# Attention feeding two mixtures of experts: tail scores in two equal parts, the feature map's minimum on GpSimd, and a fused last pair

## The chip, the cores and the metric

The kernel runs on one core of one Trainium2 chip. The metric is the device time of one execution in microseconds (us); the median of three runs of the kernel before is 1090.05 us (1089.28 to 1090.55). PE is the matrix engine, ACT the scalar engine, DVE the vector engine, POOL is GpSimd, and SP issues the transfers.

## The reference

Four batches of eight heads, 576 positions of 64 numbers. Each head mixes local causal attention with a read from a memory matrix; the result, 2304 tokens of 512, goes through two mixtures of experts.

```python
scores = scale * np.matmul(q, k.transpose(0, 1, 3, 2))      # causal mask, softmax -> a
local = np.matmul(a, v)
def phi(x):
    return np.where(x > 0, x, np.exp(x) - 1.0) + 1.0
q_p = phi(q)
mem_out = (q_p @ M_prev) / ((q_p @ z_prev)[..., None] + 1e-06)
x = g * mem_out + (1 - g) * local
# soft mixture: logits = x @ phi; softmax over the tokens -> slots; 8 experts; softmax over the slots -> back
# second mixture: 8 Sinkhorn rounds on the gate, then all 8 experts on all 2304 tokens
```

The feature map phi is x + 1 for positive x and exp(x) otherwise.

## The kernel before

**Stages.** Attention fills the span's first 255 us. It is followed by the first mixture, where weights stream in (255 to 294 us), and by the second, where PE is busy nearly all the time to the end.

**Pairs and steps.** Two heads make a pair; there are 16 pairs, `order[p]` for p = 0 to 15, four to a batch. The 576 queries of a pair are cut in five query tiles: four of 128 and a tail of 64, in which both heads are stacked to fill 128 rows. A step is a pair and a tile. For each step `scores` puts query times key into a bank of the accumulator memory (two products, high and low part of the operands, `kh` and `klz`), takes the smallest of the negated scores with DVE into `mn` and leaves the masked scores in `sm` (L387; the tail's in `smt`, L377), and has ACT exponentiate them in place (L394). `transposes` turns the exponentials on PE (`pt`, L437; the tail's L419 and L425) and ACT or DVE copy them into `pA` (tiles 0 and 1) and `pB` (tiles 2, 3 and the tail). `attend` multiplies them with the values (`po`, L476) and ACT copies the result to `ot`. "sm(2,1)" below is tile 2 of head 1.

**The tail's scores** are made of 576 keys in two parts, 512 and 64 keys wide (L361 to L377).

**The memory read** is prepared one pair ahead. `pre_exp` makes `qe`, the exponential of the raw query `qp` (L330, ACT), and cuts `qp` below at zero (L331, ACT); `pre_phi` adds min(`qe`, 1) to it on DVE (L336). `post_mem` multiplies with the memory (`pma`, `pmb`, L489), `post_mr` and `post_mx` divide. Two pairs ahead, `pre_qh`, `pre_ql`, `pre_kh` and `pre_kl` split queries and keys into high and low parts: the high ones on ACT (`qh`, `kh`), the remainders on POOL (`qh`, `qz`, `klz`, all L268).

**After a pair.** `post_r` makes the divisors of the softmax (`pz`, `sums`, `r`, L522 to L532), `post_x` turns `ot` back and multiplies (L541, L544), `post_add` adds the memory's part on POOL (L556), `post_t` turns x (`pxT`, copies `xT`, L566), and `post_logits` multiplies it with the slots' matrix (`pl`, L579, L585) and adds to `lt` (L592). After the fourth pair of a batch the routing follows: `route_logits` (a maximum, L598), `route_turn`, `route_max`, `route_factor`, and `route_slots` (`pu`, L687; `uacc`, L696). In the last batch `weight_sums` (`rs`, `stkr`, L671 to L674) and `slot_inputs` (`psl`, `sT`, L707) end the stage, and `ph` (L890) begins the first mixture.

**What sets the order.** A hand-written list sets the order on ACT and SP: for each step scores, transposes, attend, with further work put in at a number n of a pair (15 numbers to a pair, `at(p, n, f)`, numbers from `POS`). The table `LATE` holds exponentials back behind a later copy. On PE, DVE and POOL a scheduler sets the order from the same program. `qe` and `xT` share one buffer (tag `sc`).

Of the kernel before, what the change touches and what calls it, by code (L numbers as in the profile page):

```python
# [21 lines left out]
def infini_attention_soft_moe_sinkhorn_moe(  # L22
# [22 lines left out]
    P = 128  # L45
# [66 lines left out]
    with ExitStack() as actx:  # L112
# [18 lines left out]
        nc.vector.memset(zero, 0.0)  # L131
        maskt = e2.tile([P, TAIL], BF16, name="maskt")
        nc.gpsimd.memset(maskt, 0.0)
        for j in range(2):
            sl = maskt[64 * j : 64 * j + 64]
# [131 lines left out]
        def remainder(e, out, x, hi):  # L267
            (nc.gpsimd if e == "P" else nc.vector).tensor_tensor(  # L268
                out=out, in0=x, in1=hi.bitcast(F32), op=ALU.subtract
            )  # L270
# [40 lines left out]
        def pre_kl(X, h, c0=0, c1=S, e=None):  # L311
            X.kl = klz[X.p % 2]
            sl = slice(D * h, D * h + D)
            remainder(
                e or ("DP" if X.p == 1 else CFG["e_kl"])[h], X.kl[sl, h, c0:c1], X.kd[sl, h, c0:c1], X.kh[sl, h, c0:c1]
            )


        def pre_exp(X):
            X.qe = e5.tile([P, S], F32, tag="sc", name="qe")  # L320
# [11 lines left out]
            nc.gpsimd.memset(X.qp[:, S:], 0.0)  # L332

        def pre_phi(X):
            x = X.qp[:, 0:S]
            nc.vector.scalar_tensor_tensor(  # L336
                out=x, in0=X.qe, scalar=1.0, in1=x, op0=ALU.min, op1=ALU.add
            )

# [5 lines left out]

        LATE = {(0, 0): 4, (0, 1): 4, (1, 1): 0, (2, 1): 1, (3, 0): 2, (3, 1): 2}

# [6 lines left out]
        def scores(X, i):  # L354
            last = i == NT - 1
            n = P * (i + 1) if not last else S
            for h in range(1 if last else 2):
                sm = smt if last else e2.tile([P, 4 * P], F32, tag="sm", name="sm", bufs=SMB)
                mnc = X.mn[:, i, h : h + 1]
                if last:  # L360
                    parts = ((0, 4 * P), (4 * P, S))  # L361
                    pss = [pst("ps") for _ in range(2)]
# [11 lines left out]
                    mn2 = X.mn[:, NT, 0:1]  # L374
                    for c, msk in ((0, zero.to_broadcast([P, 4 * P])), (1, maskt)):
# [87 lines left out]
        def attend(X, i):  # L463
# [4 lines left out]
            for n, w, o0 in ((2, 2 * P, 0), (NT, W2, 2 * P)):  # L468
                po = pst("po")
                for j in range(n):  # L470

                    c0 = P * j if n == 2 else P * max(0, j - 2)
                    for h in range(2):
                        t, o_ = (X.pA, 2 * P * j) if n == 2 else (X.pB, OB[j])
                        rhs = t[:, h, o_ : o_ + w - c0]
                        nc.tensor.matmul(  # L476
                            po[64 * h : 64 * h + 64, c0:w], X.vt[:, j, h, :], rhs,
                            start=(j == 0), stop=(j == n - 1),
                        )
                copy(CFG["e_oA" if n == 2 else "e_oB"], X.ot[:, o0 : o0 + w], po[:, 0:w])  # L480


        def post_mem(X):
# [50 lines left out]
        def post_x(X, parts):  # L534
            x1 = X.ot.rearrange("p (t c) -> p t c", t=NT)
            end = X.p == NP - 1
            for t0, t1 in parts:
# [12 lines left out]
                )  # L550
                if end:
                    nc.vector.tensor_add(X.x[:, t0:t1], X.x[:, t0:t1], x1[:, t0:t1])

# [21 lines left out]
        def post_logits(X):  # L575

            pl = pst("pl")
            for t in range(4):
                nc.tensor.matmul(  # L579
                    pl[32 * t : 32 * t + 32, 0:P], phi_sb[:, X.hp],  # L580
                    X.xT[:, P * t : P * t + P], start=True, stop=True,
                )

            for t in range(4):
                nc.tensor.matmul(  # L585
                    pl[32 * t : 32 * t + 32, P : P + TAIL], phi_sb[:, X.hp],
                    X.xT[:, 4 * P : S], start=True, stop=True,
                )
            if X.hp == 0:
                nc.vector.tensor_copy(lt, pl[:, 0 : P + TAIL])  # L590
            else:
# [4 lines left out]
        def route_logits(b):  # L596
            m5 = e4.tile([P, 1], F32, tag="m5", name="m5")
            nc.vector.tensor_reduce(out=m5, in_=lt, op=ALU.max, axis=AX.X)  # L598
            R.m5 = m5

# [75 lines left out]
        def route_slots(b):  # L676
# [7 lines left out]
            for r in range(NHP + 1):  # L684
                for g in range(4):
# [4 lines left out]
                    )  # L690
                if r == 3:
                    weight_sums(b)
# [28 lines left out]
        def at(p, n, f, *args):  # L721
# [4 lines left out]
            ("kh", pre_tiles), ("qh", pre_qh), ("ql0", pre_ql, 0), ("ql1", pre_ql, 1), ("qz", pre_qz), ("kh", pre_kh),  # L726
            ("kl0", pre_kl, 0), ("kl1", pre_kl, 1), ("exp", pre_exp), ("phi", pre_phi),
        )
# [5 lines left out]
        ROUTE = (  # L734
            ("ra", route_logits), ("rb", route_turn), ("rc", route_max), ("rd", route_factor),
            ("re", route_slots),
        )
        for p in range(NP):
# [3 lines left out]
            if p + 1 < NP:  # L742
                if p > 1:
                    at(p, POS["l1"], load_q1, p + 1)
                for nm, f, *a in PRE:
                    if not p or f in (pre_tiles, pre_exp, pre_phi):
                        at(p, POS[nm], f, pairs[p + 1], *a)
            if 0 < p < NP - 2:
                for n, f, *a in ((1, load_heads, "qd"), (2, load_heads, "kd")):
                    at(p, n, f, p + 2, *a)  # L750
            if p < NP - 2:
                for n, f, *a in (
                    (8, pre_qh), (8, pre_ql, 0), (8, pre_ql, 1), (9, pre_qz), (9, pre_kh),
                    (9, pre_kl, 0), (9, pre_kl, 1),
                ):
                    at(p, n, f, pairs[p + 2], *a)
            for n, (nm, f, *a) in enumerate(MEM):
                at(p, POS[nm] if p + 1 < NP else POS["mz"] + 2 * n, f, pairs[p], *a)
            if hp == NHP - 1 and p + 1 < NP:
# [970 lines left out]
```

## Time and profile before

| | |
|---|---|
| median of three runs | 1090.05 us |
| the profiled execution's own time | 1093.55 us |
| its span in the trace | 1091.8 us |
| mean granted clock of PE | 0.987 |
| attention, to the first `ph` | 0 to 254.75 us |
| busy share of the span: PE, POOL, DVE, ACT | 97%, 67%, 72%, 57% |

The shares are a mean over stages of different kinds: outside the attention stage PE alone, or the transfers, set the time, and the change touches only the attention stage and its end. The tail's scores begin once in each pair, so that the distance from one such start to the next is the time of a pair: 13.22 to 13.57 us in the eight pairs that have no routing near them, 15.55 to 16.68 in the three that carry a routing, 13.89 to 14.32 in the three behind those, and 13.39 in the last.

### The profile page before, as it was taken

The page shows a single profiled execution, that of the slowest core. Times are in us where ns is not written, and L with a number is a line of the kernel's source. Part 1 is how long each engine was busy: PE and PEld are TensorE (multiplying, and loading weights), DVE is VectorE, ACT ScalarE, POOL GpSimd, SP SyncE. Part 2 cuts the span into 40 slices and gives each one's busy share as a digit, 9 for nine tenths or more (in the row PEclk, how much of TensorE's full clock was granted, in tenths as well). Part 3 has the DMA queues.
Part 4 walks back from the last instruction along what each step waited for, and adds up shares of the span by engine and source line. Part 5 has one row for each costly group of instructions (what it writes and reads, how often), then busy time and mean ns, then how long its engine had stood idle before and what let it go on. Part 6 is the DMA issues. An engine that isn't in the chain of part 4 may idle for free.

```text
span 1091.8 us, 24586 instructions
## 1 busy us (share of the span) xinstructions
PE 1058.1 (97%) x9157; PEld 968.1 (89%) x9157; DVE 790.7 (72%) x1764; ACT 623.0 (57%) x1322; POOL 730.1 (67%) x683
## 2 busy tenths in 40 slices
PE   6999999988999999999999999999999999999998
PEld 4878878764477899999999999999999999999998
DVE  7888878764157466777777777777777777877776
ACT  7998989841243666456445645554564464456442
POOL 6655646400153499679678867968886796889765
PEclk9999999997989999999999999999999999999999
DMA  9476767568812014113210421321042132110211
GB/s 212 135 216 188 215 202 217 155 235 356 351 55 87 1 20 159 36 20 118 65 24 11 156 39 21 114 67 24 12 155 40 21 113 65 24 16 15 69 54 59
DMA packets 103574, 113.08 MB, mean 104 GB/s; under 512 B 69152, under 2 KB 79520, under 8 KB 99360
## 3 DMA queue, kind: packets, MB, share of 16 engines
q1 hardware_dynamic: 103024, 111.42, 33.8%
q8 instruction: 73, 1.20, 0.5%
q14 instruction: 45, 0.37, 0.1%
q10 hardware_dynamic: 432, 0.09, 0.0%
HBM read 95.74 MB, written 4.72 MB: 92 GB/s over the span
## 4 chain that ended last, share of the span: by engine, by line
PE 80%; DVE 5%; DMA 5%; ACT 4%; issue 3%; POOL 3%; SPq 0%; DVEq 0%; ACTq 0%; POOLq 0%
PE y L1530 56%; PE l L1146 5%; PE po L476 3%; PE pt L437 2%; PE y L1493 2%; DMA kd<-in_k_dram 2%; ACT sm L394 2%; PE pa L1093 2%; DMA wm<-in_moe_w_dram 2%; DMA w<-in_moe_w_dram 1%; PE ph L890 1%; PE ps L371 1%; PE ps L366 1%; DVE sm L387 1%; PE pt L419 1%
## 5 line engine op out<-in xcount | busy, mean ns | idle before, releaser
L1170 DVE SCALAR_TENSOR_TENSOR f<-l,f 128x512 f32<-128x512 f32 x268 | 183.8, 686 | 83.9 <-ACT a11h L1176 70.1
L1187 POOL TENSOR_TENSOR s1l<-f,s1h 128x512 fp32r<-128x512 f32 x67 | 87.3, 1303 | 116.6 <-ACT s1h L1176 116.6
L1544 DVE TENSOR_TENSOR accA<-accA,y 128x512 f32<-128x512 f32 x125 | 85.6, 685 | 54.0 <-PE y L1530 54.0
L1166 ACT ACTIVATE f<-l 128x512 f32<-128x512 f32 x67 | 40.1, 598 | 120.1 <-PE l L1146 119.5
L1176 ACT ACTIVATE a12h<-l 128x512 fp32r<-128x512 f32 x72 | 43.3, 601 | 103.0 <-PE y L1530 83.0
L1187 POOL TENSOR_TENSOR s4l<-f,s4h 128x512 fp32r<-128x512 f32 x67 | 87.7, 1308 | 17.3 <-PE y L1530 17.3
L1544 DVE TENSOR_TENSOR accB<-accB,y 128x512 f32<-128x512 f32 x125 | 85.7, 685 | 4.2
L1187 POOL TENSOR_TENSOR s2l<-f,s2h 128x512 fp32r<-128x512 f32 x67 | 87.6, 1307 | 1.3 <-ACT s2h L1176 0.5
L1187 POOL TENSOR_TENSOR s3l<-f,s3h 128x512 fp32r<-128x512 f32 x67 | 87.8, 1311 | 0.0
L1146 PE MATMUL l<-c4T,a 128*128 128x256 f32 x576 | 78.1, 278 | 0.0
L394 ACT ACTIVATE sm<-sm,mn 128x128 f32<-128x128 f32 (+3 forms) x128 | 70.9, 557 | 8.3 <-DVE mn L387 7.9
L1530 PE MATMUL y<-T2h,s2h 128*128 128x256 f32 x268 | 74.7, 279 | 0.0
L1530 PE MATMUL y<-T2l,s2h 128*128 128x256 f32 x268 | 74.1, 276 | 0.0
L1530 PE MATMUL y<-T2h,s2l 128*128 128x256 f32 x268 | 74.1, 276 | 0.0
L1530 PE MATMUL y<-T1h,s1h 128*128 128x256 f32 x268 | 74.0, 276 | 0.0
L1530 PE MATMUL y<-T1l,s1h 128*128 128x256 f32 x268 | 74.0, 276 | 0.0
L1530 PE MATMUL y<-T1h,s1l 128*128 128x256 f32 x268 | 74.0, 276 | 0.0
L1530 PE MATMUL y<-T4h,a22h 128*128 128x256 f32 x268 | 74.0, 276 | 0.0
L1530 PE MATMUL y<-T4l,a22h 128*128 128x256 f32 x268 | 74.0, 276 | 0.0
L1530 PE MATMUL y<-T4h,a22l 128*128 128x256 f32 x268 | 74.0, 276 | 0.0
L1530 PE MATMUL y<-BB1h,s3l 128*128 128x256 f32 x268 | 73.1, 276 | 0.9 <-POOL s3l L1187 0.9
L1530 PE MATMUL y<-BB2h,a12h 128*128 128x256 f32 x268 | 73.6, 279 | 0.0
(324 smaller groups left out, 4063.1 us busy)
## 6 DMA issues: line engine op xcount, KB each, us to landing
wm<-in_moe_w_dram SPq DMA_DIRECT2D x32, 1024.0 KB, 7.2
raw<-in_moe_w_dram SPq DMA_DIRECT2D x32, 512.0 KB, 3.6
w<-in_moe_w_dram SPq DMA_DIRECT2D x32, 512.0 KB, 5.4
qd<-in_q_dram SPq DMA_DIRECT2D x30, 288.0 KB, 4.2
kd<-in_k_dram SPq DMA_DIRECT2D x30, 288.0 KB, 4.3
c4T<-ct SPq DMA_DIRECT2D x224, 32.0 KB, 2.0
qp<-in_q_dram SPq DMA_DIRECT2D x15, 288.0 KB, 3.0
vt<-in_v_dram SPq DMA_DIRECT2D x16, 256.0 KB, 4.5
```

The source lines that it names most:

```text
L394: nc.scalar.activation(out=sm[:, 0:n], in_=sm[:, 0:n], func=AF.Exp, scale=-1.0, bias=mnc, accum_out=X.sums[:, i, h : h + 1],)
L437: nc.tensor.transpose(pt[:, o_ : o_ + P], pr[:, P * j : P * j + P], ident)
L476: nc.tensor.matmul(po[64 * h : 64 * h + 64, c0:w], X.vt[:, j, h, :], rhs, start=(j == 0), stop=(j == n - 1),)
L1093: nc.tensor.matmul(pa[32 * j : 32 * j + 32, 0:256], soT[:, c, :], w1[j][:, c, :], start=(c == 0), stop=(c == KD - 1),)
L1146: nc.tensor.matmul(ph[:, f, :], a4s[e][:, P * (KH * j + f) : P * (KH * j + f) + P], c4T[:, UT * u : UT * u + UT], start=True, stop=True,)
L1166: nc.scalar.activation(out=f_tile(g, nm), in_=ph(g, nm), func=AF.Relu)
L1170: nc.vector.scalar_tensor_tensor(out=f_tile(g, nm), in0=ph(g, src), scalar=0.0, in1=b, op0=ALU.max, op1=op)
L1176: nc.scalar.activation(out=h_tile(g, nm, "h"), in_=ph(g, nm) if a else FU[g, nm], func=AF.Relu if a else AF.Copy)
L1187: nc.gpsimd.tensor_tensor(out=lo, in0=FU[g, nm], in1=hi, op=ALU.subtract)
L1493: nc.tensor.matmul(Y[g, i], X[g, f"a{i}{j}", "hhl"[n]][:, f, :], BB[j, "hlh"[n]][:, f].rearrange("p a c -> p (a c)"), start=j == 1 and f = ...
L1530: nc.tensor.matmul(o_, a[:, f, :], b[:, f, :], start=n == 0, stop=n == 3 * KH - 1)
L1544: nc.vector.tensor_tensor(out=acc, in0=acc, in1=y, op=ALU.add)
```

## The change

- **Tail scores.** The two parts are 288 keys wide each.
- **Features.** For every pair but the first POOL puts min(`qp`, 0) into `qe` (`pre_min`), ACT exponentiates it in place, and DVE takes the larger of `qp` + 1 and `qe`. ACT's cut at zero (L331) is gone. The remainder `klz` of two pairs ahead moves from number 9 to 14 of a pair.
- **Third step.** sm(2,1) is no longer held back: both heads' exponentials of tile 2 stand together on ACT.
- **The end.** In the last pair the divisors come at number 0; turning `ot` of tiles 0 and 1 back stands inside `attend`; one DVE instruction of 64 columns for each tile and head makes product and sum (`end_x`); the copies of x go to ACT (`end_t`); the products with the slots' matrix are cut in pieces (`end_l`). The maximum of the logits is taken in the instruction that adds them (all batches); the last `weight_sums` moves ahead.

```diff
-                    parts = ((0, 4 * P), (4 * P, S))
+                    parts = ((0, SH), (SH, S))          # SH = S // 2
...
-                nc.scalar.activation(out=X.qe, in_=X.qp[:, 0:S], func=AF.Exp)
-                nc.scalar.activation(out=X.qp[:, 0:S], in_=X.qp[:, 0:S], func=AF.Relu)
+                nc.scalar.activation(out=X.qe, in_=X.qe, func=AF.Exp)
...
+        def pre_min(X):
+            X.qe = e5.tile([P, S], F32, tag="sc", name="qe")
+            nc.gpsimd.tensor_scalar(
+                out=X.qe, in0=X.qp[:, 0:S], scalar1=0.0, scalar2=None, op0=ALU.min
+            )
...
+                nc.vector.scalar_tensor_tensor(
+                    out=x, in0=x, scalar=1.0, in1=X.qe, op0=ALU.add, op1=ALU.max
+                )
...
-        LATE = {(0, 0): 4, (0, 1): 4, (1, 1): 0, (2, 1): 1, (3, 0): 2, (3, 1): 2}
+        LATE = {(0, 0): 4, (0, 1): 4, (1, 1): 0, (3, 0): 2, (3, 1): 2}
...
+                    if n == NT and j == 2 and X.p == NP - 1:
+                        end_x(X, 0, 2)
...
+        def end_x(X, t0, t1):
+            px = pst("px")
+            for t in range(t0, t1):
+                nc.tensor.transpose(
+                    px[:, P * (t - t0) : P * (t - t0) + P], X.ot[:, P * t : P * t + P], ident
+                )
+            for t in range(t0, t1):
+                for h in range(2):
+                    c0 = P * (t - t0) + D * h
+                    xs = X.x[:, t, D * h : D * h + D]
+                    nc.vector.scalar_tensor_tensor(
+                        out=xs, in0=px[:, c0 : c0 + D], scalar=X.r2[:, t, h : h + 1], in1=xs,
+                        op0=ALU.mult, op1=ALU.add,
+                    )
...
+            elif X.hp == NHP - 1:
+                R.m5 = e4.tile([P, 1], F32, tag="m5", name="m5")
+                nc.vector.tensor_tensor_reduce(
+                    out=lt, in0=lt, in1=pl[:, 0 : P + TAIL], scale=1.0, scalar=-3.0e38,
+                    op0=ALU.add, op1=ALU.max, accum_out=R.m5,
+                )
...
-                if r == 3:
+                if r == (0 if b == B - 1 else 3):
                     weight_sums(b)
...
+                for n, f in ((14, pre_min), (15, pre_exp), (15, pre_phi)):
+                    at(p, n, f, pairs[p + 1])
...
-                    (9, pre_kl, 0), (9, pre_kl, 1),
+                    (14, pre_kl, 0), (14, pre_kl, 1),
...
-                    (1, post_r), (2, post_x, ((0, 2),)), (3, post_t, ((0, 2),)),
-                    (3, post_x, ((2, 5),)), (3, post_t, ((2, 5),)), (9, post_logits),
+                    (0, post_r), (1, end_t, 0, 2), (1, end_x, 2, 5), (2, end_l, 0, 2),
+                    (2, end_t, 2, 4), (2, end_t, 4, 5), (3, end_l, 2, 4), (3, end_l, 4, 5),
+                    (9, post_logits),
```

ACT in one pair, before; from the exponentials of tile 0 and 1 to those of tile 3 (`pA` and `pB` are the copies of turned exponentials, `ot` those of the attended values):

```order
L394 ACTIVATE sm,sums<-sm,mn 128x128 x2
L330 ACTIVATE qe<-qp 128x576
L331 ACTIVATE qp<-qp 128x576
L394 ACTIVATE sm,sums<-sm,mn 128x256
L62 ACTIVATE ot<-po 128x256
L62 ACTIVATE ot<-po 128x320
L62 ACTIVATE pA<-pt 128x2x128
L394 ACTIVATE sm,sums<-sm,mn 128x256
L394 ACTIVATE sm,sums<-sm,mn 128x384
L62 ACTIVATE pA<-pt 128x2x256
L394 ACTIVATE sm,sums<-sm,mn 128x384
L62 ACTIVATE pB<-pt 128x3x128
```

The same stretch of ACT now:

```order
L406 ACTIVATE sm,sums<-sm,mn 128x128 x2
L406 ACTIVATE sm,sums<-sm,mn 128x256
L332 ACTIVATE qe<-qe 128x576
L62 ACTIVATE ot<-po 128x256
L62 ACTIVATE ot<-po 128x320
L62 ACTIVATE pA<-pt 128x2x128
L406 ACTIVATE sm,sums<-sm,mn 128x256
L406 ACTIVATE sm,sums<-sm,mn 128x384 x2
L62 ACTIVATE pA<-pt 128x2x256
L62 ACTIVATE pB<-pt 128x3x128
```

The cut at zero is gone, the exponential of the features stands behind one more exponential of scores, and the 512 wide copy to `pA` stands behind the second 384 wide exponential where it stood ahead of it.

POOL in one pair, before:

```order
L268 TENSOR_TENSOR qz_150<-qd,qz_150 64x64 x2
L268 TENSOR_TENSOR qh<-qd,qh 64x512 x2
L268 TENSOR_TENSOR klz_157<-kd,kh 64x576 x2
L343 MEMSET sums 128x2
L556 TENSOR_TENSOR x<-x,ot 128x640
L467 MEMSET ot 128x64
```

And now:

```order
L269 TENSOR_TENSOR qz_150<-qd,qz_150 64x64 x2
L269 TENSOR_TENSOR qh<-qd,qh 64x512 x2
L337 TENSOR_SCALAR qe<-qp 128x576
L269 TENSOR_TENSOR klz_157<-kd,kh 64x576 x2
L355 MEMSET sums 128x2
L606 TENSOR_TENSOR x<-x,ot 128x640
```

The minimum stands between the remainders of the queries and those of the keys, which both come later by its time.

PE at the end of the stage, before, from the last attended values to the logits:

```order
L476 MATMUL po<-pB,vt 64x320 x6
L476 MATMUL po<-pB,vt 64x192 x2
L476 MATMUL po<-pB,vt 64x64 x2
L522 MATMUL pz<-sums,ident 64x1
L541 MATMUL px<-ident,ot 128x128 x2
L566 MATMUL pxT<-ident,x 128x128 x2
L541 MATMUL px<-ident,ot 128x128 x3
L566 MATMUL pxT<-ident,x 128x128 x3
L579 MATMUL pl<-xT,phi_sb 32x128 x4
```

And now (`pz` stands ahead of the first attended values):

```order
L488 MATMUL po<-pB,vt 64x320 x6
L500 MATMUL px<-ident,ot 128x128 x2
L488 MATMUL po<-pB,vt 64x192 x2
L488 MATMUL po<-pB,vt 64x64 x2
L518 MATMUL pxT<-ident,x 128x128
L500 MATMUL px<-ident,ot 128x128 x2
L518 MATMUL pxT<-ident,x 128x128
L500 MATMUL px<-ident,ot 128x128
L525 MATMUL pl<-xT,phi_sb 32x128 x2
L518 MATMUL pxT<-ident,x 128x128 x3
L525 MATMUL pl<-xT,phi_sb 32x128 x2
```

The first two tiles' `px` stands among the last attended values, and the transposes of x are spread among the others.

## Rows read from the trace of the kernel before

**Rows 1.** Busy time by stretch: span, PE, PEld, DVE, ACT, POOL (instructions), clock, DMA share, GB/s.

```profile
100.00:125.00 25.00, 24.07 (x220) 20.24 (x219) 20.34 (x74) 23.25 (x63) 15.66 (x19) 1.00 0.69 205
```

**Rows 2.** Timeline, PE: start us, us, engine, line, operation [idle before <- releaser].

```profile
115.01 0.55 PE L437 MATMUL pt<-ident,sm 128*128 128x128 f32 x3 [0.51 <-ACT sm L394]
115.32 0.71 PE L366 MATMUL ps<-kh,qz 128*128 128x512 f32 x2
...
116.33 0.30 PE L366 MATMUL ps<-kh,qz 128*128 128x64 f32 x2
...
116.69 0.92 PE L489 MATMUL pma<-mbd,qp 128*128 128x130 f32 x6
```

**Rows 3.** Timeline, ACT, the same pair.

```profile
107.05 0.27 ACT L62 ACTIVATE pB<-pt 128x128 f32<-128x128 f32 x1
107.68 0.66 ACT L62 ACTIVATE pB<-pt 128x384 f32<-128x384 f32 x2 [0.36 <-PE pt L419]
...
109.76 0.68 ACT L331 ACTIVATE qp<-qp 128x576 f32<-128x576 f32 x1
...
113.38 0.58 ACT L62 ACTIVATE pA<-pt 128x512 f32<-128x512 f32 x1
114.25 0.61 ACT L394 ACTIVATE sm<-sm,mn 128x384 f32<-128x384 f32 x1 [0.29 <-DVE mn L387]
...
117.02 1.04 ACT L62 ACTIVATE qh<-qd 128x1024 fp32r<-128x1024 f32 x1
```

**Rows 4.** Timeline, POOL, the same pair.

```profile
105.63 2.62 POOL L268 TENSOR_TENSOR qh<-qd,qh 64x512 fp32r<-64x512 f32 x2
108.21 2.90 POOL L268 TENSOR_TENSOR klz<-kd,kh 64x576 fp32r<-64x576 f32 x2
```

**Rows 5.** Timeline, DVE, the same pair.

```profile
108.47 0.41 DVE L387 CUSTOM_DVE_ANT_0 sm<-ps,maskw 128x256 f32<-128x256 f32 x1
...
109.14 0.51 DVE L528 TENSOR_SCALAR r<-sums,gB 128x5 f32<-128x5 f32 x1
110.47 1.25 DVE L336 SCALAR_TENSOR_TENSOR qp<-qe,qp 128x576 f32<-128x576 f32 x1 [0.82 <-ACT qp L331]
```

**Rows 6.** Timeline, DVE and POOL, in a pair that carries a routing.

```profile
97.22 0.76 DVE L336 SCALAR_TENSOR_TENSOR qp<-qe,qp 128x576 f32<-128x576 f32 x1 [1.20 <-ACT qp L331]
...
99.02 0.10 POOL L343 MEMSET sums<- 128x2 f32 x1 [3.17 <-DVE r L528]
```

**Rows 7.** Groups by line and form, POOL, 0 to 320 us: count | busy us, mean ns | idle before.

```profile
L268 POOL TENSOR_TENSOR klz<-kd,kh 64x576 fp32r<-64x576 f32 x29 | 40.9, 1411 | 1.3
...
L332 POOL MEMSET qp<- 128x64 f32 x16 | 2.4, 148 | 1.9 <-PE pmb L489 1.8
...
L880 POOL MEMSET hT<- 128x224 f32 x2 | 0.5, 285 | 20.3 <-PE pu L687 20.3
```

**Rows 8.** The tile qp, its transfers, 0 to 250 us.

```profile
DMA to landing us min/median/max: 2.7/3.0/9.4
```

**Rows 9.** Timeline, DVE, a pair behind a routing.

```profile
91.17 0.98 DVE L528 TENSOR_SCALAR r<-sums,gB 128x5 f32<-128x5 f32 x1
```

**Rows 10.** Timeline, end of the attention stage: ACT, PE and DVE; then the chain.

```profile
237.94 0.44 ACT L62 ACTIVATE ot<-po 128x320 f32<-128x320 f32 x1 [1.61 <-PE pz L522]
...
239.73 0.44 PE L566 MATMUL pxT<-ident,x 128*128 128x128 f32 x2 [1.41 <-DVE x L552]
...
241.90 0.52 PE L566 MATMUL pxT<-ident,x 128*128 128x128 f32 x3 [1.41 <-DVE x L552]
...
252.48 1.89 PE L707 MATMUL psl<-stkr,uacc 128*128 128x32 f32 x8 [1.42 <-DVE stkr L674]
...
243.91 0.35 DVE L592 TENSOR_TENSOR lt<-lt,pl 128x192 f32<-128x192 f32 x1 [0.96 <-PE pl L585]
...
264.40 16.50 DMA wm<-in_moe_w_dram
```

**Rows 11.** Busy time by stretch, columns as in Rows 1.

```profile
243.00:248.00 5.00, 3.09 (x26) 2.01 (x27) 2.06 (x9) 0.46 (x2) 0.00 (x0) 0.50 1.01 423
```

More of the change, by code (lines that the diff above doesn't have):

```diff
@@ L313, in pre_kl @@
             sl = slice(D * h, D * h + D)
-            remainder(
+            i = remainder(
                 e or ("DP" if X.p == 1 else CFG["e_kl"])[h], X.kl[sl, h, c0:c1], X.kd[sl, h, c0:c1], X.kh[sl, h, c0:c1]
             )
+            if X.p > 1:
+                tc.keep_in_program_order(i)
         def pre_exp(X):
-            X.qe = e5.tile([P, S], F32, tag="sc", name="qe")
             if X.p == 0:
+                X.qe = e5.tile([P, S], F32, tag="sc", name="qe")
                 for h in range(2):
@@ L329, in pre_exp @@
             else:
-                nc.scalar.activation(out=X.qe, in_=X.qp[:, 0:S], func=AF.Exp)
-                nc.scalar.activation(out=X.qp[:, 0:S], in_=X.qp[:, 0:S], func=AF.Relu)
+                nc.scalar.activation(out=X.qe, in_=X.qe, func=AF.Exp)
             nc.gpsimd.memset(X.qp[:, S:], 0.0)
+        def pre_min(X):
+            X.qe = e5.tile([P, S], F32, tag="sc", name="qe")
+            nc.gpsimd.tensor_scalar(
+                out=X.qe, in0=X.qp[:, 0:S], scalar1=0.0, scalar2=None, op0=ALU.min
+            )
         def pre_phi(X):
             x = X.qp[:, 0:S]
-            nc.vector.scalar_tensor_tensor(
-                out=x, in0=X.qe, scalar=1.0, in1=x, op0=ALU.min, op1=ALU.add
-            )
+            if X.p == 0:
+                nc.vector.scalar_tensor_tensor(
+                    out=x, in0=X.qe, scalar=1.0, in1=x, op0=ALU.min, op1=ALU.add
+                )
+            else:
+                nc.vector.scalar_tensor_tensor(
+                    out=x, in0=x, scalar=1.0, in1=X.qe, op0=ALU.add, op1=ALU.max
+                )
         def pre_tiles(X):
@@ L374, in scores @@
                     mn2 = X.mn[:, NT, 0:1]
-                    for c, msk in ((0, zero.to_broadcast([P, 4 * P])), (1, maskt)):
+                    for c, msk in ((0, zero.to_broadcast([P, SH])), (1, maskt)):
                         c0, c1 = parts[c]
@@ L479, in attend, with end_t, end_l @@
                         )
+                    if n == NT and j == 2 and X.p == NP - 1:
+                        end_x(X, 0, 2)
                 copy(CFG["e_oA" if n == 2 else "e_oB"], X.ot[:, o0 : o0 + w], po[:, 0:w])
+        def end_x(X, t0, t1):
[8 more added lines that the diff above has]
+                    xs = X.x[:, t, D * h : D * h + D]
+                    nc.vector.scalar_tensor_tensor(
+                        out=xs, in0=px[:, c0 : c0 + D], scalar=X.r2[:, t, h : h + 1], in1=xs,
+                        op0=ALU.mult, op1=ALU.add,
+                    )
+        def end_t(X, t0, t1):
+            if t0 == 0:
+                X.xT = e5.tile([P, S], F32, tag="sc", name="xT")
+                X.pl = pst("pl")
+            px = pst("pxT")
+            for t in range(t0, t1):
+                nc.tensor.transpose(px[:, P * (t - t0) : P * (t - t0) + P], X.x[:, t], ident)
+            a, z = P * t0, min(P * t1, S)
+            copy("A", X.xT[:, a:z], px[:, 0 : z - a])
+        def end_l(X, t0, t1):
+            for t in range(t0, t1):
+                if t < 4:
+                    nc.tensor.matmul(
+                        X.pl[32 * t : 32 * t + 32, 0:P], phi_sb[:, X.hp],
+                        X.xT[:, P * t : P * t + P], start=True, stop=True,
+                    )
+                    continue
+                for j in range(4):
+                    nc.tensor.matmul(
+                        X.pl[32 * j : 32 * j + 32, P : P + TAIL], phi_sb[:, X.hp],
+                        X.xT[:, 4 * P : S], start=True, stop=True,
+                    )
         def post_mem(X):
@@ L535, in post_x @@
             x1 = X.ot.rearrange("p (t c) -> p t c", t=NT)
-            end = X.p == NP - 1
             for t0, t1 in parts:
@@ L550, in post_x @@
                 )
-                if end:
-                    nc.vector.tensor_add(X.x[:, t0:t1], X.x[:, t0:t1], x1[:, t0:t1])
         def post_add(X):
@@ L575, in post_logits @@
         def post_logits(X):
[L577 to L588, printed above, removed]
+            if X.p < NP - 1:
+                X.pl = pst("pl")
+                end_l(X, 0, NT)
+            pl = X.pl
             if X.hp == 0:
                 nc.vector.tensor_copy(lt, pl[:, 0 : P + TAIL])
+            elif X.hp == NHP - 1:
[3 more added lines that the diff above has]
+                    op0=ALU.add, op1=ALU.max, accum_out=R.m5,
+                )
             else:
@@ L594, in post_logits @@
                 )
[L596 to L599, printed above, removed]
         def route_turn(b):
@@ L757, in infini_attention_soft_moe_sinkhorn_moe @@
             for n, (nm, f, *a) in enumerate(MEM):
-                at(p, POS[nm] if p + 1 < NP else POS["mz"] + 2 * n, f, pairs[p], *a)
+                at(p, POS[nm] if p + 1 < NP else (11, 13, 14, 14)[n], f, pairs[p], *a)
             if hp == NHP - 1 and p + 1 < NP:
```

13 lines of the change are left out of this document (7 added, 6 removed).

## The prediction

> **What bounds the kernel now.** I first read the stretches: in the attention stage PE is busy for 24.07 of 25 us, ACT for 23.25, DVE for 20.34 [rows 1]. No engine has room, so I read one pair's timeline engine by engine and look for PE's idle time. There is one gap: before the turn of sm(2,1), at 115.01, PE stands 0.51 us and is released by that exponential [rows 2]. ACT itself had idled 0.29 for DVE's minimum [rows 3]. Going back on DVE, the features' instruction (L336) waits 0.82 us for ACT's cut at zero and then takes 1.25 [rows 5], and everything behind it on DVE up to sm(2,1) is late by it. I call T the start of the turn of sm(2,1): 101.73 in the pair shown (the next, 115.01, less the pair's 13.28), and count all offsets from it.
>
> Why 1.25? In another pair the same instruction took 0.76, with POOL idle for the 3.17 us up to 99.02 [rows 6]. In the pair shown POOL's `klz` run from 108.21 to 111.11 [rows 4]; the features' instruction begins at 110.47 and ends 0.61 behind them, the short `r`, begun at 109.14, ends at 109.65, as the first `klz` does. So DVE instructions that read only SBUF stand still until the POOL instruction under way has ended, and get in between two of them.
>
> Ahead of the first mixture the end of the stage is one chain in which PE twice waits 1.41 us for DVE [rows 10]; behind it the transfers set the time (a wait of 16.50 for weights, rows 10), then PE.
>
> **The change part by part** (us of the profiled execution, 1093.55, which is 3.5 above the median; I take differences against it and put them on the median).
>
> *Tail in halves.* 1.37 now, from 115.32 to 116.69: 1.01 for four products of 512 columns, 0.36 for four of 64 [rows 2]. Eight of 288 at 1.01/2048 us a column are 1.14. PE saves 0.2; it is used below.
>
> *ACT.* The cut at zero, 0.68, goes. But the 512 wide `pA` copy, now done while ACT waits for sm(2,1) (113.38, rows 3), comes behind it. Before, `qh` began at 117.02, T + 2.01; with the copy's 0.49 it begins at T + 2.5 and ends at T + 3.54. The single 128 wide `pB` copy shifts from T + 5.32 to 5.81 and ends at 6.08; PE's scores of sm(1,0) need the bank that it frees. They hardly waited for it; now they slip by up to 0.43, and with them DVE's minimum of sm(1,0), done at 108.88 or T + 7.15 [rows 5], to 7.58; its exponential, now ahead of the features' one, takes 0.49 to T + 8.1, and the features' one 0.68 to about T + 8.75. (Before, the cut at zero ended at T + 8.7, from rows 3.) So the engine's gain of 0.68 is spent before it reaches DVE.
>
> *POOL.* `qh`'s remainders began at T + 3.9; the tail is 0.2 earlier, but they need ACT's `qh`: T + 3.6, ended at T + 6.18 (2.58 long, rows 4). Then comes the minimum, of length m, then the two `klz` of 1.45 each: to T + 7.63 + m and T + 9.08 + m. The trace has no one-input arithmetic on POOL. Bounds for m: the memsets, 148 ns at 64 and 285 at 224 elements, give 0.86 ns an element and 0.59 at 576; the two-input remainder took 1.41 [rows 7]. It reads one stream, so I take 0.65, near the memset; the bounds stay for the range. Queued behind it on POOL are `klz`, on SP the next keys' load that waits for `klz`; neither is used before the next pair but one.
>
> The Trainium skill (GPSIMD Engine Reference, section 3.1) gives POOL 1.03 cycles an element where it copies or has one input, against 2.6 for two. By that ratio the 1.41 would become an estimated 0.56, and the sum of the next paragraph 0.26 a pair instead of 0.35.
>
> *The features on DVE.* The exponential is ready at T + 8.75, the first `klz` ends at T + 8.28 for m = 0.65: DVE misses the space between the two and stands until T + 9.73, ends 0.61 later at T + 10.34; before it ended at 111.72, T + 9.99. From there to the turn of sm(2,1) it is the same chain, 111.72 to 115.01, 3.29. The pair becomes 13.63 instead of 13.28: +0.35 (0.29 for m = 0.59; just over m = 1.1 DVE gets in between, but is then held at its next `r`, +0.4 to +0.8). ACT and PE alone, by the offsets above, would stay at about 13.3. For the eight plain pairs that is **+2.8**.
>
> The Trainium skill (SBUF — State Buffer, section Who interferes with whom) says that DVE's second pair of ports is GpSimd's, under an exclusive lock. The trace agrees (0.76 alone, 1.25 beside `klz`); without a lock the features would end at T + 9.5 and the pair go by ACT's loop, 13.3.
>
> *Late queries.* `qp` is issued when the memory read is done with its buffer, at about T + 3.1, and lands after 2.7 to 9.4, median 3.0 [rows 8]: at T + 6.1, just ahead of the minimum. ACT needed it at T + 7.3 before. A landing of 4 us now costs a pair 0.9; for a few such pairs **+0.5**, at most 2.
>
> *Pairs behind a routing.* There `r` stood 0.98 behind POOL's `qh` [rows 9], ahead of the copies of xT that PE needs. Now these copies come first on DVE. I count 0.6, 0.25 and 0.25 for the three (13.9 to 14.3 now, and no shorter than a plain pair) and nothing for the new wait, since other things are late there: **-0.9** in all, between +0.5 and -1.5. The three routing pairs end in waits for the slots' turn: 0. The last pair has no `klz`: **-0.2**.
>
> *The end.* Both idle times of 1.41 go. In their place the copy of `ot`, 0.44, is on the path [rows 10]; the ten fused instructions of 64 columns are four beside `po` and six in the open. Their length is bounded by the `lt` sum (192 columns, 0.35) and the slope from it to the features' 0.76 at 576: 0.21 to 0.35 each, 1.3 to 2.1 for six, about what the product and the sum in the second 1.41 take, which they replace. So `lt` begins 2.3 earlier, at 241.6. `psl` waited 1.42 for `stkr` [rows 10]; that is now ready with the first half of `uacc`, 0.7 earlier. **-3.0**, bounds -2 to -4. The clock was 0.50, the lower of PE's levels, from 243 on, just behind the two idle times [rows 11]. If denser work kept it up a little longer, `psl` (1.89) and what precedes it could gain up to 1.5; I take **-0.3**. The weights' transfers that follow are released by `plt` and `ph`, which come earlier by the same 2 to 3, and the queue is empty for a while behind 256, so the gain passes.
>
> *Sum:* 2.8 + 0.5 - 0.9 - 0.2 - 3.0 - 0.3 = -1.1: 1089.0 by the median.
>
> **The rivals.**
>
> *The relief of ACT arrives (0.32).* The features' exponential gets ready 0.5 earlier than I count, or the minimum gets under way while `qp` waits, and DVE slips in between the `klz`. Then the features end 1.4 earlier, the pair falls back to ACT's own loop, 13.2 to 13.3, and the eight pairs give 0 to -1: with the rest -4 to -6, about 1085.5. For it: 0.47 out of sums of 8 us decide. Against it: the exponential of sm(1,0) stands ahead.
>
> *The minimum is a heavy instruction (0.19).* With m of 0.9 to 1.1, or 1.4 as in rows 7, the pair grows by 0.6 to 0.8, the eight by 4.8 to 6.4, and late queries add 1: +1.5 to +4, about 1092.5, slower. It decides from m = 0.85 on if DVE still misses the space.
>
> *The end's gain is swallowed (0.11).* If the weights behind 256.6 wait for something that doesn't move, -3.0 becomes -0.7, and the sum is +1.3 to +2.5: 1092.
>
> *The fused end doesn't do what it says:* ten small DVE instructions at 0.35 and PE's transposes waiting for each give back 1; that lies inside the first two cases.
>
> **How the numbers follow.** A measurement of this kernel tells 0.2%, 2.2 us, from no change. The forecast, 0.38, spans 1085.5 to 1092.5 with the bounds of its terms (m, the pairs behind a routing, late queries, the end's -2 to -4): 0.12 of it faster, 0.20 same, 0.06 slower. The first rival is faster nearly throughout (0.30, and 0.02 same), the second slower 0.14 and same 0.05, the third slower 0.05 and same 0.06. That gives faster 0.42, same 0.33, slower 0.25. The range leaves out the outer part of the first rival (the end at -4 with pairs at 13.2) and of the second (m = 1.1 with a weak end), a tenth each: 1084 to 1094.
>
> **What would show it.** Right: `klz` later by 0.6 to 0.7 in each pair, the features' instruction on DVE over 1.2 long and ending with the second `klz`; PE's gap at sm(2,1) at 0.8 or so; plain pairs of 13.6; `lt` and `psl` 2.3 and 3 closer to the last `po`. Wrong: features of 0.76, plain pairs under 13.3 (first rival); a minimum of 0.9 or more (second); `ph` 3 earlier but the last weights landing as before (third).

## The result, and the profile after

The changed kernel takes 1105.75 us (median of four runs, 1103.85 to 1107.71) against 1090.3 before: 1.0138 of it, 95% interval 1.011 to 1.0166. The profiled execution took 1104.45 with a span of 1102.7, 10.9 longer than before's. I had forecast 1089.0 and a range to 1094.

The tail starts tell where it went. The first came at 17.12 instead of 18.77, the last at 247.69 instead of 229.74, so the pairs lost 18. From there to the first `ph` of the mixture it is 20.95 instead of 25.01, so the end gained 4. The plain pairs are of two kinds now: three of the eight take 13.8 to 14.0, the others 14.96 to 16.70; the three that carry a routing take 18.66, 17.71 and 19.12. Behind the first `ph` the profiled execution is 3 shorter than before's (834.1 and 837.1), which lies within what that stretch differs by from run to run.

Busy time by stretch, the changed kernel, columns as in [rows 1]: PE 22.61 of 25, where it had 24.07, and ACT 19.80, where it had 23.25. DVE and POOL are a little fuller than before (20.96 for 20.34 and 16.16 for 15.66), and neither is full, so the pairs wait.

```profile
100.00:125.00 25.00, 22.61 (x195) 18.53 (x193) 20.96 (x74) 19.80 (x57) 16.16 (x17) 1.00 0.64 178
```

POOL's timeline over two pairs of the changed kernel (start, length; compare [rows 4]):

```profile
112.28 2.62 POOL L269 TENSOR_TENSOR qh<-qd,qh 64x512 fp32r<-64x512 f32 x2 [0.26 <-ACT qh L62]
114.88 1.65 POOL L337 TENSOR_SCALAR qe<-qp 128x576 f32<-128x576 f32 x1
116.49 3.31 POOL L269 TENSOR_TENSOR klz<-kd,kh 64x576 fp32r<-64x576 f32 x2
...
126.27 2.62 POOL L269 TENSOR_TENSOR qh<-qd,qh 64x512 fp32r<-64x512 f32 x2 [0.25 <-ACT qh L62]
130.21 1.65 POOL L337 TENSOR_SCALAR qe<-qp 128x576 f32<-128x576 f32 x1 [1.32 <-DMA qp<-in_q_dram]
131.82 3.29 POOL L269 TENSOR_TENSOR klz<-kd,kh 64x576 fp32r<-64x576 f32 x2
```

Two things stand here. The minimum takes 1.65, more than the two-input remainders of the same width (1.41, [rows 7]). And in the second pair it waits 1.32 us for the queries. The first of these pairs took 13.98, the second 15.31. Over the stage, the group of the minima shows 17.4 us of waiting ahead of them (busy, mean ns | idle before, releasers), and the queries' landing time has gone from a median of 3.0 [rows 8] to 4.6:

```profile
L337 POOL TENSOR_SCALAR qe<-qp 128x576 f32<-128x576 f32 x15 | 24.7, 1648 | 17.4 <-DMA qp<-in_q_dram 9.6 <-PE po L488 4.6 <-DVE mn L399 2.9
```

```profile
DMA to landing us min/median/max: 2.8/4.6/8.8
```

SP's timeline of the changed kernel says why (issue time, DMA): keys, values and a weight piece of 1 MB go out from 119.83 on, because the keys' load waits for `klz`; the queries are issued 2.98 behind the piece and land just before 130.21, where they release the minimum. In the pair of before (the last two lines) the piece went out 4.2 ahead of the queries.

```profile
119.83 1.25 SPq L208 DMA_DIRECT2D kd<-in_k_dram  x2
121.18 0.53 SPq L228 DMA_DIRECT2D vt<-in_v_dram  x1
...
122.36 0.58 SPq L99 DMA_DIRECT2D wm<-in_moe_w_dram  x1
125.34 0.33 SPq L221 DMA_DIRECT2D qp<-in_q_dram  x1
```

```profile
113.88 0.58 SPq L99 DMA_DIRECT2D wm<-in_moe_w_dram  x1
118.09 0.33 SPq L220 DMA_DIRECT2D qp<-in_q_dram  x1
```

DVE's timeline of the first pair (compare [rows 5]): the features' instruction begins at 117.27, beside the first `klz`, ends 0.6 behind it, and the next short `r` stands until the second `klz` has ended (0.83 instead of 0.22).

```profile
117.27 1.25 DVE L348 SCALAR_TENSOR_TENSOR qp<-qp,qe 128x576 f32<-128x576 f32 x1 [0.72 <-ACT qe L332]
...
119.00 0.83 DVE L581 TENSOR_SCALAR r<-sums,gB 128x5 f32<-128x5 f32 x1
```

PE's timeline of the same pair (compare [rows 2]): a new gap of 0.41 ahead of sm(1,0), for the 128 wide `pB` copy, and the old one ahead of the turn of sm(2,1), 0.87 instead of 0.51. The tail itself, 122.88 to 124.03, takes 1.15 instead of 1.37.

```profile
114.71 0.39 PE L397 MATMUL ps<-kh,qh 128*128 128x256 f32 x1 [0.41 <-ACT pB L62]
...
122.58 0.55 PE L449 MATMUL pt<-ident,sm 128*128 128x128 f32 x3 [0.87 <-ACT sm L406]
122.88 0.52 PE L378 MATMUL ps<-kh,qz 128*128 128x288 f32 x2
...
124.03 0.83 PE L542 MATMUL pma<-mbd,qp 128*128 128x130 f32 x6
```

At the end of the stage, DVE's fused instructions and the chain of the changed kernel (compare [rows 10]): six of 64 columns take 1.24 together; `lt` stands 12.05 behind the last tail start, where it stood 14.17 behind it.

```profile
255.63 0.86 DVE L507 SCALAR_TENSOR_TENSOR x<-px,r,x 128x64 f32<-128x64 f32 x4 [1.63 <-PE px L500]
257.42 1.24 DVE L507 SCALAR_TENSOR_TENSOR x<-px,r,x 128x64 f32<-128x64 f32 x6 [0.92 <-PE px L500]
```

```profile
259.74 0.35 DVE lt L634
...
267.21 1.06 PE psl L749 x8
...
268.64 8.81 PE ph L935 x64
277.47 17.23 DMA wm<-in_moe_w_dram
```

### The profile page after: what moved, and what is told of

It is laid out like the page before. It is cut to its first block, busy times and chain, and to the rows that moved or that the text cites. A ratio compares the mean times of both kernels' runs of the same rounds, so it can differ in the third digit from the quotient of the medians.

```text
span 1102.7 us, 24656 instructions
## 1 busy us (share of the span) xinstructions
PE 1057.9 (96%) x9157; PEld 965.9 (88%) x9157; DVE 798.5 (72%) x1768; ACT 611.9 (55%) x1310; POOL 761.0 (69%) x698
## 4 chain that ended last, share of the span: by engine, by line
PE 72%; DVE 7%; DMA 6%; POOL 5%; issue 5%; ACT 4%; SPq 0%; POOLq 0%; DVEq 0%; ACTq 0%
PE y L1575 56%; PE l L1191 5%; DMA qp<-in_q_dram 3%; DMA wm<-in_moe_w_dram 2%; DVE qp L348 2%; POOL qe L337 2%; DVE sm L399 1%; ACT sm L406 1%; PE pt L449 1%; PE pa L1138 1%; DMA w<-in_moe_w_dram 1%; PE po L488 1%; PE y L1538 1%; DVE r L581 1%; PE ph L935 1%
```

## The experiments

The theory after this reading is "length": the minimum on POOL, far longer than I took it to be, delays `klz`, and through `klz` both DVE and SP's queue. The first rival is "ACT order": sm(2,1) no longer held back, and the `pA` copy behind it, cost the time. Two more came up later: that the place of the minimum costs and not its length, and that the queries are late for another reason than the queue.

All times in us; the last column is the ratio to executions of before on the same chip, with its 95% interval. Tail starts and plain pairs are read off PE's records of each profile, the spans off the cores' view. "Plain pair" is the length that repeats in the middle of the stage; the first pairs of a run can differ (from the first to the second tail start e10 takes 15.84).

| run | first tail | plain pair | last tail | span | ratio to before |
|---|---|---|---|---|---|
| before | 18.77 | 13.29 | 229.74 | 1091.8 | 1 |
| changed | 17.12 | 13.8 to 16.7 | 247.69 | 1102.7 | 1.0138 (1.011 to 1.0166) |
| e1: features back | 16.91 | 13.49 | 225.10 | 1083.2 | 0.9957 (0.9931 to 0.9982) |
| e2: features only | 18.93 | 13.2 to 15.9 | 244.10 | 1105.2 | 1.0159 (1.0116 to 1.0202) |
| e3: end only | 19.20 | 13.29 | 231.56 | 1090.6 | 0.9981 (0.9957 to 1.0005) |
| e4: minimum on DVE | 16.75 | 13.66 | 230.15 | 1085.3 | 0.9987 (0.9965 to 1.001) |
| e6: weights behind queries | 16.83 | 13.98 | 231.27 | 1091.2 | 0.9993 (0.9961 to 1.0025) |
| e7: halves and end | 18.11 | 13.01 | 224.27 | 1079.3 | 0.9926 (0.9897 to 0.9954) |
| e8: halves only | 18.67 | 13.01 | 225.07 | 1084.4 | 0.9926 (0.989 to 0.9962) |
| e9: halves, end, weights behind | 18.35 | 13.01 | 225.33 | 1084.0 | 0.9914 (0.9881 to 0.9948) |
| e10: half minimum | 16.64 | 13.38 | 227.79 | 1086.6 | 0.996 (0.9931 to 0.9988) |
| e11: e6, third step held back | 19.01 | 13.81 | 232.09 | 1092.4 | 0.9999 (0.9972 to 1.0026) |

**e1, the features as before, the rest changed.** The diff in part: `pre_min` goes too, DVE's instruction takes its old form, and `klz` is no longer kept in program order on POOL, which the features' part of the change also does.

```diff
-                nc.scalar.activation(out=X.qe, in_=X.qe, func=AF.Exp)
+                nc.scalar.activation(out=X.qe, in_=X.qp[:, 0:S], func=AF.Exp)
+                nc.scalar.activation(out=X.qp[:, 0:S], in_=X.qp[:, 0:S], func=AF.Relu)
...
-                    (14, pre_kl, 0), (14, pre_kl, 1),
+                    (9, pre_kl, 0), (9, pre_kl, 1),
```

> The changed kernel with the features and the keys' remainder as before (exponential and cut at zero on ACT, klz at number 9); tail halves, third step together and the fused end stay. Theory 'length' (the minimum on POOL, 1.65 us long, is what costs): plain pairs of 13.1 to 13.3, the last tail start at 226 to 230, the stage behind it 4 shorter than before, the time 1084 to 1087, 3 to 6 faster than before. Rival 'ACT order' (third step's exponentials together and the later pA copy cost): plain pairs of 13.6 or more, last tail start at 235 or later, time 1090 to 1096.

Last tail start 225.1, ratio 0.9957: all that was lost, and more, comes back, so the features' part is the loss. The plain pairs are 13.49, though, above the 13.3 of the theory and near the rival's 13.6. PE's timeline has the wait that the order on ACT makes:

```profile
118.31 0.39 PE L386 MATMUL ps<-kh,qh 128*128 128x256 f32 x1 [0.41 <-ACT pB L62]
125.69 0.55 PE L438 MATMUL pt<-ident,sm 128*128 128x128 f32 x3 [0.41 <-ACT sm L395]
```

**e2, the features' part alone** (e1's diff the other way, on the kernel before).

> The kernel before with the features' part alone (minimum on POOL, klz at number 14). Theory 'length': minimum of 1.65 in each pair, plain pairs of 13.9 to 15.3, queries landing late in several, last tail start 15 to 20 later than before, time 12 to 20 slower. Rival 'ACT order': the features alone cost less than half, last tail start less than 8 later, time less than 8 slower.

1.0159, last tail 14.4 later than before: just under the 15 to 20 that "length" had, and far over the 8 of the rival. "ACT order" alone falls.

**e3, the fused end alone** (`end_x`, `end_t`, `end_l`, the maximum in the logits' sum, the earlier `weight_sums`, on the kernel before).

> The kernel before with the fused end (and the maximum in the logits' sum) alone. If the gain passes the transfers' stage: first ph 4 earlier (250.7), end 3.5 to 4.5 earlier, time 1085.5 to 1087. If the transfers' stage swallows it: first ph 4 earlier but the last weights before the second mixture land as before, time 1089 to 1090. Pairs ahead of the end are 13.3 as before by either.

From the last tail start to the first `ph` it is 21.36 instead of 25.01; from there to the first `pa`, the end of the transfers' stage, 37.2 instead of 38.0 (37.2 to 38.1 over all runs). So up to the first `pa` the transfers swallow nothing. In the time only 0.2% is seen, with an interval to 1.0005, less than the 3.5 to 4.5 us expected. In the profiled execution the stretch from the first to the second tail start took 14.7, 1.4 longer than before's, and from the first `pa` to the end the profiles differ, 795 to 801, without any pattern that I can name. The size of the end's gain is read off the stage; in the time no run shows it.

**e4, the minimum on DVE.**

```diff
-            nc.gpsimd.tensor_scalar(
+            nc.vector.tensor_scalar(
                 out=X.qe, in0=X.qp[:, 0:S], scalar1=0.0, scalar2=None, op0=ALU.min
```

> The changed kernel with the minimum on DVE in place of POOL, all else as changed. Theory 'length': klz follow qh at once, the keys' loads go out as before, no late queries; DVE's minimum takes 0.4 to 0.6 and the features' instruction stands behind the second klz: plain pairs of 13.3 to 13.6, last tail start at 229 to 234, time 1085 to 1090. Rival 'place' (klz's number 14 and the order on ACT cost, not the minimum's time on POOL): pairs of 13.9 and more, late queries remain, time above 1098.

Plain pairs 13.66, a little above the theory's, no late queries, ratio 0.9987 with 1 in its interval. Number 14 and the order on ACT are all as in the changed kernel; only POOL is free of the minimum. The rival "place" falls as far as POOL's time is concerned. The expected 0.4 to 0.6 for DVE's minimum was missed: it takes 1.56 in a plain pair, where the first `klz` runs from 122.13 to 123.54 beside it, and 0.45 in the last pair, which has no `klz`.

```profile
122.31 1.56 DVE L337 TENSOR_SCALAR qe<-qp 128x576 f32<-128x576 f32 x1
```

```profile
223.38 0.45 DVE L337 TENSOR_SCALAR qe<-qp 128x576 f32<-128x576 f32 x1
```

**e5, what POOL's instructions take.**

> Nothing of the reference is computed: two query tiles are loaded, and POOL runs single instructions on 128 rows of float32, twice each: the minimum with a constant at 576, 288 and 64 columns, then at 576 the maximum, sum, product, minimum and sum in one, copy, two-input difference and product, memset. Then DVE runs the two-input features' instruction at 576, twice alone and eight times beside four POOL instructions of one kind (minimum, copy, difference, memset). Theory 'one slow operation': the minimum takes 1.65 at 576 and sum, product and copy 0.5 to 0.7. Theory 'any one-input arithmetic with a constant is slow on POOL': sum and product take 1.6 too, only copy and memset 0.6. Theory 'float32 on POOL costs per element': the minimum at 288 takes 0.85, at 64 0.25. Lock: DVE's 0.76 stretches to about its own time plus the rest of the POOL instruction beside minimum, copy and difference; beside memset it may not.

Groups by form of this run (count | busy us, mean ns), and the first minimum of 576 columns from its timeline:

```profile
3.72 1.65 POOL L80 TENSOR_SCALAR pout<-qa 128x576 f32<-128x576 f32 x1 [3.28 <-DMA qa<-in_q_dram]
```

```profile
L87 POOL COPY po<-d 128x576 f32<-128x576 f32 x4 | 4.3, 1087 | 2.4 <-DVE d L111 2.2
...
L102 POOL TENSOR_TENSOR pout<-qa,za 128x576 f32<-128x576 f32 x2 | 2.8, 1395 | 0.2
...
L80 POOL TENSOR_SCALAR pout<-qa 128x288 f32<-128x288 f32 x2 | 1.8, 924 | 0.2
...
L101 POOL COPY pout<-qa 128x576 f32<-128x576 f32 x2 | 1.3, 663 | 0.1
L104 POOL MEMSET pout<- 128x576 f32 x2 | 1.2, 578 | 0.1
L80 POOL TENSOR_SCALAR pout<-qa 128x64 f32<-128x64 f32 x2 | 0.7, 364 | 0.2
```

Minimum, maximum, sum and product with a constant took 1.65 to 1.66 each, and 2.14 for two operations in one instruction. So it is any of these four with a constant, at 2.5 ns a column and 0.2 on top (1.65, 0.92 and 0.36 at 576, 288 and 64); copy and memset take 0.66 and 0.58. The Trainium skill (GPSIMD Engine Reference, section 3.1) gives 1.03 cycles an element for up to two operations; the prediction's estimate from it, 0.56, comes near the copy's 0.66 and not near the minimum; the measurement decides. Beside four of POOL's differences eight features' instructions took 10.23, where one alone takes 0.76. A copy of 64 columns on POOL, begun beside six of them in a row, ended only behind the last of them. The memsets ran from 69.12 on, when DVE stood still, so this run doesn't show whether a memset is held or holds:

```profile
52.72 10.23 DVE L119 SCALAR_TENSOR_TENSOR e<-d,za 128x576 f32<-128x576 f32 x8
...
64.87 4.09 DVE L119 SCALAR_TENSOR_TENSOR e<-d,za 128x576 f32<-128x576 f32 x6
65.02 4.04 POOL L115 COPY po<-d 128x64 f32<-128x64 f32 x1 [4.69 <-DVE d L111]
69.12 2.48 POOL L91 MEMSET po<- 128x576 f32 x4
71.64 0.69 DVE L123 TENSOR_TENSOR acc<-acc,po 128x512 f32<-128x512 f32 x1 [2.67 <-POOL po L91]
```

The delay goes both ways: the copies of 576 columns took 1.09 beside DVE, 0.66 alone, and the changed kernel's `klz` 1.62 on the mean, 1.41 before.

**e6, the weight piece behind the queries.** One number in the table of positions:

```diff
-'lw': 20
+'lw': 25
```

> The changed kernel, with the mixture's weight piece of each pair issued behind the queries' load (number 25 instead of 20) in place of ahead of it. Theory 'late queries come from the queue': klz's delay puts the keys' load, the values and the weight piece just ahead of the queries, which then land late; with the piece behind them, POOL's wait for the queries falls from 9.6 to under 3, all plain pairs come to 13.9 to 14.1, the last tail start 5 to 8 earlier than in the changed kernel (240 to 243), time 1097 to 1101. Rival 'the queries are late for their own issue': wait and pairs stay, time 1104 to 1107.

The piece ahead of the queries is the cause, and more of it than expected: the landing median goes from 4.6 to 2.8, the wait ahead of the minimum from 17.4 to 2.8, all plain pairs come to 13.83 to 13.99, the last tail start comes 16.4 earlier, and the ratio to before goes from 1.0138 to 0.9993 (12 us by the medians, 16 by the ratios). All that the change had lost against before is this one collision; what the minimum costs beside it, the rest of the change pays for. Whether the queries wait their turn in the queue or share the transfer engines with the piece, the run doesn't tell.

```profile
DMA to landing us min/median/max: 2.6/2.8/8.3
```

```profile
L337 POOL TENSOR_SCALAR qe<-qp 128x576 f32<-128x576 f32 x15 | 24.7, 1644 | 2.8 <-PE pt L431 2.7
```

**e7, halves and end, without the features and with sm(2,1) held back.** Against e1 only this line is new:

```diff
+        LATE = {(0, 0): 4, (0, 1): 4, (1, 1): 0, (2, 1): 1, (3, 0): 2, (3, 1): 2}
```

> The kernel before with the tail in halves and the fused end only (features, klz and the held-back sm(2,1) as before). Theory 'the later pA copy costs ACT 0.2 a pair': plain pairs fall from the 13.49 of the run with the features back to 13.0 to 13.2, last tail start 222 to 225, time 1082 to 1086. Rival 'the halves cost': plain pairs stay at 13.45 to 13.5, time 1087 to 1090. Third possibility, both hold each other up: first pair begins 1.9 earlier in either case.

Plain pairs 13.01, 0.48 under e1: that is what "third step together" costs where ACT still has the cut at zero. At the first pair it is the other way: with sm(2,1) not held back the first tail starts 1.2 earlier (16.91 against 18.11); the third possibility's 1.9 in either case was not met (0.7 here, against before's 18.77). The kernel is 0.9926 of before.

**e8, the halves alone.** The diff in part: the masks take the parts' width.

```diff
-                    parts = ((0, 4 * P), (4 * P, S))
+                    parts = ((0, SH), (SH, S))
```

> The kernel before with the tail's scores in halves alone. The run with the halves and the fused end had plain pairs of 13.01 and its last tail start 5.5 earlier than before. Theory 'the halves shorten every pair': plain pairs of 13.0 to 13.1, the last tail start 4 to 6 earlier than before (224 to 226), time 3.5 to 6 faster. Rival 'only the tail's 0.2 on PE, off the path': plain pairs 13.2 to 13.3, time within 2 of before.

13.01 again, last tail 4.7 earlier, ratio 0.9926: the halves alone are as good as halves and end within what can be told. PE's timeline shows that the gap ahead of sm(2,1) is down from 0.51 to 0.41 and that the tail (113.80 to 114.94) takes 1.14 instead of 1.37; together that is 0.33 for the pair's 0.28, so the tail lies on the path:

```profile
113.50 0.55 PE L438 MATMUL pt<-ident,sm 128*128 128x128 f32 x3 [0.41 <-ACT sm L395]
113.80 0.51 PE L367 MATMUL ps<-kh,qz 128*128 128x288 f32 x2
...
114.94 0.27 PE L490 MATMUL pma<-mbd,qp 128*128 128x130 f32 x1
```

**e9, e7 with the weight piece behind the queries.**

> The kernel before with the halves, the fused end, and the weight piece behind the queries' load (number 25). Theory 'the queue costs only where queries are needed early': without the minimum queries have 1 us to spare, so the time is within 2 of the run without the move (7 faster than before). Rival 'the piece ahead of the queries always costs': pairs that still have late queries shrink, last tail start 2 or more earlier than 224.3, time 2 to 4 faster again.

0.9914 beside e7's 0.9926, the same pairs: without the minimum the piece ahead of the queries costs nothing that can be told. This is the best of the kernels in the median, though not told apart from e7 and e8.

**e10, half a minimum,** on e6. POOL's line of the edit; ACT's exponential is halved likewise, and DVE reads the half twice:

```diff
-                out=X.qe, in0=X.qp[:, 0:S], scalar1=0.0, scalar2=None, op0=ALU.min
+                out=X.qe[:, 0:SH], in0=X.qp[:, 0:SH], scalar1=0.0, scalar2=None, op0=ALU.min
```

> The changed kernel with the weight piece behind the queries, and POOL's minimum and ACT's exponential over the first 288 columns only; DVE uses them for both halves of the features, so the second half's features are of other numbers. With the full width this gave plain pairs of 13.98. The minimum takes 0.92 instead of 1.65, the exponential 0.3 less. Theory 'its length ahead of klz sets the pair': plain pairs of 13.3 to 13.6, last tail start 4 to 6 earlier (225 to 227.5). Rival 'its place does' (a new instruction between qh and klz, whatever its length): plain pairs stay at 13.8 to 14.0.

Plain pairs 13.38, 0.60 under e6 for a minimum 0.72 shorter (926 ns): "length" holds, "place" falls. The last tail start, 227.79, lies just behind the 225 to 227.5 expected, by the 15.84 of the first stretch. The shorter exponential is not what gained: it ends at 123.25, and with e6's 0.69 it would have ended at 123.50, still ahead of the features' start at 123.59. Here DVE gets in between the two `klz` and the features take 0.75:

```profile
121.34 0.92 POOL L337 TENSOR_SCALAR qe<-qp 128x288 f32<-128x288 f32 x1
122.24 3.37 POOL L269 TENSOR_TENSOR klz<-kd,kh 64x576 fp32r<-64x576 f32 x2
```

```profile
122.81 0.44 ACT L332 ACTIVATE qe<-qe 128x288 f32<-128x288 f32 x1
```

```profile
123.59 0.75 DVE L350 SCALAR_TENSOR_TENSOR qp<-qp,qe 128x576 f32<-128x576 f32 x1
```

**e11, e6 with sm(2,1) held back.**

> The changed kernel with the weight piece behind the queries and sm(2,1) held back as before. The held-back order takes away PE's wait of 0.41 for the pB copy ahead of sm(1,0). Theory 'two waits in a row on one path' (PE's scores of sm(1,0) start ahead of all that DVE and ACT do later in the pair): plain pairs fall from 13.98 by 0.4 to 13.5 to 13.6, last tail start 4 to 6 earlier than 231.3, time 1086 to 1089. Rival 'the minimum on POOL is the path, from the memory read on': its wait takes over, PE's gap at sm(2,1) grows from 0.88 to 1.3, plain pairs stay at 13.9 to 14.0, time as before the change.

13.81: only 0.17 of the 0.41 comes back, so neither had it whole. The rival was nearer with the pair, but not with PE's gap at sm(2,1), which it had at 1.3 and which is as long as in e6 (0.87). PE's wait for the `pB` copy is gone; in its place ACT now waits 0.25 for POOL's minimum before the features' exponential, which begins 7.78 behind the turn of sm(2,1) where in e6 it began 7.95 behind it (123.48 after 115.53). That 0.17 is the pair's gain: with the long minimum the path runs over POOL.

```profile
117.46 0.55 PE L449 MATMUL pt<-ident,sm 128*128 128x128 f32 x3 [0.87 <-ACT sm L406]
```

```profile
125.24 0.68 ACT L332 ACTIVATE qe<-qe 128x576 f32<-128x576 f32 x1 [0.25 <-POOL qe L337]
```

## Why the prediction was wrong, step by step

Summed over the last tail start, the runs give: halves -4.7 (e8 to before), run to run -0.8 (e8 to e7, which differ in the end alone), third step together +0.8 (e1 to e7), features with queries on time +6.2 (e6 to e1), late queries +16.4 (changed to e6): together +18.0, the shift measured. Behind the last tail start -4.1. With the queries on time (e6) the last tail start is 1.5 later than before, where the forecast for the pairs without its late queries was +1.7 (2.8 - 0.9 - 0.2). That this agrees is luck: the features cost more than forecast, and the halves, which the sum had at nothing, paid for it.

- **Late queries: the step that failed.** I had +0.5, at most 2; it was 16.4 at the last tail start, and 12 to 16 in the time. The arithmetic of one late landing was right (a landing 1.32 us late cost a pair 1.33); wrong was the sentence on what is queued behind the minimum, `klz` on POOL and the keys' load on SP: "neither is used before the next pair but one". True of the keys; but behind the keys' load, on the same queue, stand the values and a weight piece of 1 MB, and they move into the window in which the queries, just made urgent by the minimum, are transferred. I had followed the wait one link and not what stood behind it. The longer minimum has its share in this, since it sets how late `klz` ends; whether 0.65 would have brought the collision too no run shows.
- **The minimum's length.** I took 0.65, between 0.59 and 1.41; it is 1.65, outside both bounds. The lower bound was a memset, the upper an instruction with twice the inputs, and neither bounds arithmetic with a constant. The estimate of 0.56 leaned the same way. e5 shows it; e10 gives 0.60 a pair for 0.72 of it.
- **The features' price by the lock.** For m over 1.1 the text had "DVE gets in between, but is then held at its next `r`, +0.4 to +0.8". DVE is held just so in these rows, and the pair is 13.98 against 13.29, +0.69. That the size fits is in part luck: by the runs it is features +0.49 (e6 to e1), third step +0.48 (e1 to e7) and halves -0.28 (e8), and the text had priced only the first. The second rival had the mechanism and the total for a pair; its 1092.5 failed with the late queries, to which it gave 1 us.
- **ACT.** The scores of sm(1,0) were to "slip by up to 0.43": PE's new gap is 0.41. The features' exponential was to be ready at T + 8.75 and was at T + 8.64 (117.23, with T = 108.59), so the gain of 0.68 is spent. But the minimum, which ends at 116.53, holds that exponential about as long as ACT's order does. e1 to e7, 0.48 a pair, is the price of the order where the cut at zero remains.
- **Tail in halves.** 0.2 a pair was the right size for the tail (1.37 to 1.15), but I let it vanish into the pair's sum and priced it at nothing by itself. Alone it takes 0.28 off a plain pair and 0.7% off the time: the largest gain in the change, hidden under the loss.
- **Pairs behind a routing.** -0.9 forecast; from e6 the three take 13.55, 14.07 and 14.00 where before they had 14.32, 13.89 and 13.89: -0.5 with the long minimum. In e7 they take 14.10, 13.13 and 13.14, -1.7, by the halves. The term can't be told apart from the others. The last pair, forecast at -0.2, came 0.6 shorter in e6 and 0.4 by the halves alone.
- **The end.** `lt` 2.1 earlier (2.3 forecast), `psl` 3.2 (3.0), `ph` 4.1 in the changed kernel and 2.8 to 3.7 in the others that have the fused end. Of the -0.3 for the clock nothing is shown to be the fused end's doing: `psl` took 1.06 in the changed kernel and e3 and 1.90 in the seven others with the fused end, but 1.06 in e2 too, which has none. The six fused instructions took 1.24, just under the bound of 1.3. That the gain passes the transfers was right up to the first `pa`, so the third rival's mechanism falls; in the time e7 and e8 have the same ratio, with the end and without.
- **The first rival** (relief of ACT arrives) needed DVE to get in early; of the kernels with the minimum on POOL only e10, with half of it, has that in all its plain pairs, at 13.38.

## What to carry to other kernels

When a wait is lengthened, follow the queue behind the waiting instruction to its end: each transfer that it holds back starts later, and has to be laid against every transfer that the same change makes urgent. An operation that no trace shows is not bounded by the nearest rows of other kinds; where the whole case hangs on its price, a forecast should carry a bound well beyond them. And parts of a change that are added up in one sum should be priced one by one: here one part, alone, was worth 0.7%, and the part meant to relieve an engine cost twice that.

## What the runs showed of the hardware that I had not expected

- POOL's arithmetic with a constant on float32 (minimum, maximum, sum, product) takes 1.65 at 128x576, longer than a two-input difference (1.395), and two and a half times a copy (0.663). DVE took 0.45 for the same minimum with POOL out of the way (e4).
- The hold between DVE and POOL goes both ways: copies 0.663 alone and 1.087 beside DVE's two-input instructions. It can last over several instructions: a copy of 64 columns stood 4.04, through six on DVE.
- The landing of a 288 KB load depended on where a 1 MB transfer stood in the order of issue: median 2.8 with it behind the load (e6) and 4.6 with it ahead, in the pair shown by 2.98 (changed). In before, with it ahead by 4.2 in the pair shown, it was 3.0.
